# Retention attention into a gated two-layer MLP on one core: another loading, another split of small work between engines, and another order

## The chip, the cores and the metric

The kernel runs on one core of a Trainium2 chip. A core has five engines with a queue of instructions each: TensorE (PE, with its weight loads listed as PEld), VectorE (DVE), ScalarE (ACT), GpSimd (POOL) and SyncE (SP, which here only starts transfers). Each queue is worked off strictly in order, and the engines wait for each other through semaphores. SP, ACT and POOL can start transfers between DRAM and the on-chip memory SBUF; TensorE writes its results to eight banks of PSUM, from which DVE and ACT read them. The metric is the device time of one execution in microseconds.

## The reference

The first half is a linear recurrence per batch (4) and head (8), over 768 tokens with heads of 64 elements. Its output, regrouped to 512 features per token, goes through a second half:

```python
for t in range(S):                                   # gamma_h = 1 - 2**(-5-h)
    state = gamma * state + k[:, :, t] (outer) v[:, :, t]
    y[:, :, t] = q[:, :, t] . state / 8
x = y regrouped to (batch, token, 512);  x_prev = x one token earlier (0 at the first)
xk = mu_k * x + (1 - mu_k) * x_prev;   xr = mu_r * x + (1 - mu_r) * x_prev
k  = relu(xk @ w_k)                                  # 512 -> 1024
out = sigmoid(xr @ w_r) * ((k * k) @ w_v)            # 1024 -> 512
```

## The kernel before

The 4 x 768 tokens are cut into 12 blocks of 256 tokens, numbered 0 to 11, three to a batch. Within a block the recurrence is done in chunks: scores between the tokens of a chunk, a causal mask, the product with the scaled v, and a state (64 x 64 per head) carried from chunk to chunk and from block to block.

All work is written out by hand. A long string ORDER names every step, and a loop at the end of the kernel issues the steps in this order, so ORDER fixes the queue of every engine. A word is `code.block.part`, then `~engine` where the step can run on several engines (v = DVE, a = ACT, p = POOL, s = SP), and `@banks` for the PSUM banks. The codes:

- `lq`, `lk`, `lv`: load of a block's q, k, v. From POOL, q and k are turned to f16 by the transfer itself. Two loads of block 0 come from SP as f32 (the tuple EARLY) into room that the key results of blocks 1 and 2 use later, and `cq`, `ck` turn them to f16. Block 0's q and k are loaded in two halves of four heads each.
- `vs`: v times the decay, in f16 (`scale_v`, L255). `Tq`, `Tk`: transposes on TensorE (L274 with whole 128-row inputs, L280 in 64x64 pieces); `Eq`, `Ek`: their copies from PSUM to SBUF on ACT (L243).
- `S`: scores (L320, L333, L341); `M`: the mask, on DVE (L349, L356); `C`: the state's products (L368, L386, L397); `U`: running sums of the state (L421); `G`: their decay; `I`, `J`: the part of y that comes from the carried state (L443); `Y`: the part within the chunk (L464, L480, L491).
- `D`: y out of PSUM, scaled by the table gy, into xT (`yout`, L509 and L516, DVE); `dx`: x minus x_prev (`differ`, L531); `X.n.w.j`: xk (w = 0) or xr (w = 1) of a quarter of the features, from dx, mu and x_prev (`mixed`, L560, DVE).
- `K`: keys (L574, L584); `Qa`, `Qb`: relu and square on ACT (L593, L601, L605); `R` and `s`: gate and sigmoid (L614, L620); `V`: values (L626); `O`: the product with the gate (L632, DVE); `st`: the store from SP (L639). `wk`, `wr`, `wv` load weights, each w_k and w_v in two halves. `z`: products of zeros on TensorE that nobody reads (L693, L700). `gy` fills the table gy in two parts. `t` (`weighed`) is a step that no word of the ORDER before uses.

A block has one of three forms. Blocks in HALF (5 to 11) go through scores and states in chunks of 64 tokens, 64x64 at a time: one word S, one M, four U. Blocks in WIDE (2, 3, 4) use chunks of 128 tokens in layout "token p and token p+128" : two words S, two M, two U. Blocks 0 and 1 use chunks of 128 with neighbouring tokens in a row. Blocks in WHOLE (0 to 5) are transposed 128 rows at a time, the others in 64x64 pieces. GROUPS joins blocks 3 and 4, 6 and 7, 9 and 10 for the second half: one X and one K serve both.

POOL's loads are started one after another (some 0.9 us each on POOL), and in the trace never more than eight of them are under way: the next is issued when the one eight before it has landed.

Of the kernel before, what the change touches and what calls it, by code (L numbers as in the profile page):

```python
# [31 lines left out]
X.1.0.1 z.1@3 K.0.3@7 X.1.0.2 Qa.0.3 K.0.2@1 X.1.0.0 Qa.0.2 X.1.0.3 Tk.2@6 K.0.1@0 Ek.2~a vs.2~v  # L32
S.2.0@67 S.2.1@45 M.2.0~v Qb.0.3 K.1.1@1 K.1.2@2 Qa.0.1 Qb.0.2 lv.3~p C.2@0 Qa.1.2 Tq.3@3 Eq.3~a
U.2.0 I.2@67 Tk.3@0 Qa.1.1 K.1.0@2 Tq.4@1 X.1.1.0 Ek.3~a Qa.1.0 M.2.1~v Y.2 lq.5~p Eq.4~a S.3.0@45
J.2 X.1.1.1 Qb.1.0 Qb.1.2 X.1.1.2 X.1.1.3 S.3.1@23 lv.4~p K.1.3@0 Qa.1.3 Qb.1.3 wv.0~p X.0.1.3
X.0.1.2 R.0.0@1 D.2~v dx.2~v X.2.0.2 Qb.0.1 s.0.0 X.2.0.0 lq.6~p R.0.1@6 s.0.1 Tk.4@0 X.2.0.3
R.1.1@7 X.2.0.1 vs.3~p M.3.0~v Ek.4~a K.2.3@1 Qa.2.3 K.2.0@6 Qa.2.0 M.3.1~v S.4.1@45 M.4.1~v
Tq.5@1 Eq.5~a C.3@23 U.3.0~v U.3.1 s.1.1 vs.4~v R.1.0@6 s.1.0 G.3~a K.2.1@0 I.3@45 Qb.2.3 S.4.0@23
M.4.0~v Y.3 C.4@67 U.4.0 U.4.1 G.4~a K.2.2@1 Qb.1.1 I.4@23 J.3 Qa.2.1 Qa.2.2 Y.4 Qb.2.0 D.3~v
V.0.0.0@6 Tq.6@45 J.4 dx.3~v V.1.1.0@7 D.4~v dx.4~v X.3.0.1 V.0.1.0@0 V.1.0.0@1 X.2.1.2 Qb.2.2  # L40
wv.1~p V.0.0.1 Eq.6~a V.0.1.1 lq.7~p lk.6~p Tk.6@45 Ek.6~a O.0.0 Tq.7@23 Eq.7~a V.1.0.1 S.6@45
lk.5~p Tk.5@6 X.3.0.2 X.3.0.3 X.3.0.0 K.3.3@2 Qb.2.1 K.3.2@3 O.1.0 Ek.5~a O.0.1 X.3.1.1 M.6~v
lv.5~p vs.5~v K.3.5@0 Qa.3.5 Qa.3.3 K.3.4@6 V.1.1.1 Qa.3.2 lv.6~p C.5@01 S.5@45 Qa.3.4 vs.6~v
C.6@23 Qb.3.3 Qb.3.2 O.1.1 M.5~v U.5.0 X.2.1.3 U.5.1 U.6.0~a U.6.1 U.6.2 U.5.2 U.6.3 K.3.0@6
X.2.1.1 Qa.3.0 Qb.3.0 V.2.0.0@7 K.3.6@4 Qa.3.6 K.3.7@6 st.0.1 Qa.3.7 Qb.3.7 I.5@01 I.6@45 V.2.0.1
K.3.1@3 Qa.3.1 Qb.3.1 X.2.1.0 R.2.0@6 lk.8~p Tk.8@23 lv.7~p Y.5 X.3.1.0 vs.7~v X.3.1.3 Y.6 X.3.1.2
s.2.0 R.3.1@6 D.5~v dx.5~v st.1.1 st.0.0 Ek.8~a X.5.0.3 O.2.0 X.5.0.0 V.2.1.0@2 X.5.0.1 R.3.0@3
D.6~v G.6~a Qb.3.4 s.3.0 s.3.1 lv.8~p R.2.1@0 s.2.1 X.5.1.3 X.5.0.2 R.4.0@1 s.4.0 V.2.1.1 lk.7~p
C.7@67 O.2.1 lk.9~p Tk.9@01 Ek.9~a lv.11~s Tk.7@45 Ek.7~a lq.8~p U.7.0 U.7.1 U.7.2 st.2.0 vs.8~v
K.5.1@3 dx.6~v Qa.5.1 K.5.2@2 I.7@45 S.7@01 U.7.3 K.5.0@6 M.7~v lv.9~p Qb.3.6 Qa.5.0 K.5.3@3  # L50
Qa.5.2 Qb.5.0 R.4.1@6 lk.11~p Qb.3.5 vs.9~v V.4.1.0@7 X.5.1.1 C.8@01 Y.7 D.7~v dx.7~v X.6.0.3
X.6.0.0 lq.11~p Qa.5.3 Qb.5.2 Tq.8@23 X.6.0.2 V.4.1.1 s.4.1 V.4.0.0@6 Eq.8~a V.3.1.0@2 Qb.5.3
Qb.5.1 V.4.0.1 X.6.0.1 lq.9~p G.7~a V.3.0.0@3 V.3.1.1 V.3.0.1 U.8.0 K.6.3@4 Qa.6.3 O.4.0 K.6.1@5
Qa.6.1 Qb.6.1 K.6.2@6 Qa.6.2 lq.10~p O.3.1 U.8.1 st.1.0 X.5.1.0 X.5.1.2 lk.10~p U.8.2 I.8@01 O.3.0
st.2.1 Tq.9@23 Eq.9~a O.4.1 Qb.6.3 S.8@45 M.8~v K.6.0@7 K.6.6@6 Qa.6.0 Qb.6.0 Qa.6.6 X.6.1.3
S.9@23 st.3.1 Tq.11@45 Y.8 Eq.11~a X.6.1.2 R.5.1@7 s.5.1 K.6.7@6 Qb.6.2 K.6.4@4 Qa.6.4 M.9~v D.8~v
dx.8~v X.8.0.0 X.8.0.3 X.8.0.1 X.8.1.1 V.5.0.0@5 R.5.0@7 K.6.5@4 s.5.0 X.6.1.1 Tk.10@01 Qa.6.7
lv.10~p vs.10~v X.6.1.0 C.9@23 U.9.0~v Ek.10~a st.3.0 Tq.10@67 V.5.0.1 O.5.0 X.8.0.2 V.5.1.0@0
R.6.1@1 Qa.6.5 U.9.1 U.9.2 U.9.3 Eq.10~a V.5.1.1 st.5.0 O.5.1 s.6.1 Qb.6.4 S.10@45 I.9@67 C.10@23
G.9~a vs.11~v U.10.0 U.10.1 U.10.2 Qb.6.5 M.10~v st.5.1 R.6.0@1 s.6.0 R.7.0@0 s.7.0 K.8.1@1 Qa.8.1  # L60
K.8.2@2 Qa.8.2 C.11@01 I.10@45 U.10.3 Y.9 K.8.0@3 D.9~v Qb.6.7 K.8.3@2 st.4.1 Tk.11@67 G.10~a
U.11.0 U.11.1 Qa.8.0 Ek.11~a U.11.2 Y.10 D.10~v R.7.1@3 s.7.1 dx.9~v dx.10~v X.9.1.1 I.11@01
X.8.1.0 S.11@67 M.11~v X.9.0.0 Qb.8.2 V.7.0.0@4 Qa.8.3 X.9.0.2 X.9.0.1 V.7.1.0@5 V.6.0.0@3 X.9.0.3
Qb.8.1 Qb.6.6 V.6.1.0@2 V.7.1.1 X.8.1.2 V.7.0.1 V.6.0.1 V.6.1.1 K.9.5@6 K.9.7@7 Qb.8.0 st.4.0
Qa.9.5 O.6.0 Y.11 O.7.1 X.8.1.3 R.8.1@6 D.11~v dx.11~v Qa.9.7 Qb.9.7 K.9.3@5 Qb.9.5 X.11.1.3
X.11.0.1 O.6.1 X.9.1.3 V.8.1.0@7 X.9.1.2 V.8.0.0@3 X.11.0.2 st.6.1 K.9.4@0 Qa.9.4 Qb.9.4 K.9.6@1
Qa.9.6 K.9.0@2 X.9.1.0 K.9.2@0 Qa.9.2 Qb.8.3 X.11.0.3 Qb.9.2 X.11.0.0 Qa.9.3 X.11.1.0 K.9.1@1
R.9.1@0 Qa.9.1 Qb.9.1 X.11.1.2 V.8.0.1 K.11.1@5 O.7.0 Qa.11.1 R.8.0@4 V.8.1.1 Qb.9.3 s.8.0
R.10.0@5 K.11.0@1 st.6.0 Qa.9.0 Qb.9.0 st.7.1 K.11.2@2 st.7.0 R.9.0@4 Qa.11.0 Qb.9.6 Qb.11.0
Qb.11.1 X.11.1.1 O.8.0 K.11.3@1 s.9.1 V.9.1.0@3 V.10.1.0@0 s.8.1 O.8.1 st.8.1 R.11.1@6 V.9.0.0@7  # L70
Qa.11.3 V.11.0.0@1 s.10.0 Qa.11.2 Qb.11.2 R.10.1@2 V.9.1.1 O.9.1 V.10.1.1 s.10.1 O.10.1 st.9.1
Qb.11.3 V.9.0.1 st.10.1 s.11.1 Vc.11.1.1@2 s.9.0 V.10.0.0@6 O.9.0 R.11.0@0 V.11.0.1 st.8.0 st.9.0
s.11.0 Oc.11.1.1 sc.11.1.1~a O.11.0 st.11.0 V.10.0.1 O.10.0 st.10.0 Vc.11.1.0@0 Oc.11.1.0
# [716 lines left out]
```

## Time and profile before

| | |
|---|---|
| time, median of 3 runs (lowest, highest) | 156.21 us (155.82, 156.54) |
| span of the profiled execution | 154.9 us |
| granted TensorE clock in it | 1.000 |
| busy: PE, DVE, ACT, POOL | 146.0, 126.9, 99.4, 55.5 us |

The span runs from the first to the last instruction of the program; the time of a run is 1.3 us longer than this span. A busy PE is not a PE at its full pace, because a matmul counts from its start until its modelled end, and the ends overlap the next starts. The pace is read from the distance of starts instead.

### The profile page before, as it was taken

Reading aid. Unit: us, or ns where it says so; the run is one execution under the profiler, and the core shown is the slowest. Engines: PE = TensorE matmul, PEld = TensorE weight load, DVE = VectorE, ACT = ScalarE, POOL = GpSimd, SP = SyncE. Lnnn points to the kernel's source line nnn. Section 1 sums busy time; section 2 is a strip of 40 time slices with the busy share of each in tenths; the row PEclk is TensorE's granted clock in tenths of the full one; section 3 lists DMA queues with packets and bytes.
Section 4 is the critical chain, followed back from the end, with each engine's and each line's share of the span. In section 5 each row is a group of like instructions: output and inputs, shape, how many; then the busy total and the mean of one; then the engine's idle time right before and its main releaser. Section 6 shows DMA issues by size and latency. Waiting matters only on the chain.

```text
span 154.9 us, 5520 instructions
## 1 busy us (share of the span) xinstructions
PE 146.0 (94%) x2423; PEld 83.9 (54%) x2423; DVE 126.9 (82%) x205; ACT 99.4 (64%) x186; POOL 55.5 (36%) x65
## 2 busy tenths in 40 slices
...
GB/s 144 263 219 194 197 228 171 196 241 218 156 180 212 199 241 258 223 234 181 116 147 204 150 68 4 4 74 203 4 4 0 6 82 136 52 0 72 96 209 169
DMA packets 45768, 22.31 MB, mean 144 GB/s; under 512 B 37416, under 2 KB 41392, under 8 KB 45744
## 3 DMA queue, kind: packets, MB, share of 16 engines
...
q10 hardware_dynamic: 448, 0.32, 0.7%
...
## 4 chain that ended last, share of the span: by engine, by line
PE 55%; DVE 24%; DMA 12%; issue 4%; POOL 3%; DVEq 0%; POOLq 0%
PE ps L626 19%; DMA v<-in_v_dram 12%; PE ps L614 9%; PE ps L574 9%; PE ps L584 8%; DVE a L356 3%; DVE xk L560 3%; DVE xr L560 3%; DVE vs L255 3%; DVE dx L531 2%; DVE xT L516 2%; DVE tg L421 2%; DVE os L632 2%; PE ps L443 2%; DVE a L349 1%
## 5 line engine op out<-in xcount | busy, mean ns | idle before, releaser
L626 PE MATMUL ps<-wv,k2s 128*128 128x512 f16 x184 | 43.4, 379 | 0.0
L593 ACT ACTIVATE kr<-ps 128x512 f32<-128x512 f32 x48 | 27.8, 596 | 23.1 <-PE ps L574 18.0
L626 PEld LDWEIGHTS <-k2s 128*128 128x128 f16 x184 | 17.4, 98 | 20.0
L632 DVE SCALAR_TENSOR_TENSOR os<-ps,rs 128x512 f32<-128x512 f32 x23 | 15.4, 683 | 14.5 <-ACT rs L620 7.4
L614 PE MATMUL ps<-wr,xr 128*128 128x512 f16 x96 | 24.1, 380 | 0.0
L584 PE MATMUL ps<-xk,wk 128*128 128x256 f16 x192 | 24.0, 273 | 0.0
L232 POOL DMA_DIRECT2D k<-in_k_dram x20 | 17.7, 898 | 15.2 <-PE ps L280 10.5
L574 PE MATMUL ps<-xk,wk 128*128 128x512 f16 x96 | 22.5, 379 | 0.0
L584 PEld LDWEIGHTS <-wk 128*128 128x128 f16 x192 | 18.1, 98 | 4.9 <-DMA wk<-in_moe_w_k_dram 0.6
L620 ACT ACTIVATE rs<-ps 128x512 f32<-128x512 f32 x24 | 13.7, 594 | 9.3 <-PE ps L614 8.9
L560 DVE SCALAR_TENSOR_TENSOR xr<-dx,mu,xT 128x256 f16<-128x256 f32 (+1 forms) x36 | 19.2, 564 | 0.1
L560 DVE SCALAR_TENSOR_TENSOR xk<-dx,mu,xT 128x256 f16<-128x256 f32 (+1 forms) x36 | 18.8, 567 | 0.2
L232 POOL DMA_DIRECT2D v<-in_v_dram x18 | 16.2, 915 | 1.4 <-DMA q<-in_q_dram 0.5
L243 ACT COPY kT<-ps 128x1024 f16<-128x1024 f16 (+1 forms) x13 | 12.2, 947 | 5.2 <-PE ps L280 4.1
L601 ACT ACTIVATE k2s<-kr 128x512 f16<-128x512 f32 x24 | 14.9, 628 | 0.3
L574 PEld LDWEIGHTS <-wk 128*128 128x128 f16 x96 | 9.2, 98 | 10.8
L531 DVE TENSOR_TENSOR dx<-xT 128x1024 f32<-128x1024 f32 x12 | 14.6, 1223 | 0.3
L605 ACT ACTIVATE k2s<-kr 128x512 f16<-128x512 f32 x24 | 14.5, 628 | 0.1
L243 ACT COPY qT<-ps 128x1024 f16<-128x1024 f16 (+1 forms) x13 | 12.3, 949 | 2.4 <-PE ps L274 2.2
L614 PEld LDWEIGHTS <-xr 128*128 128x128 f16 x96 | 8.8, 97 | 9.2 <-DVE xr L560 0.2
L255 DVE TENSOR_TENSOR vs<-v,csm_sb 128x1024 f16<-128x1024 f32 x10 | 12.1, 1216 | 2.0 <-DMA v<-in_v_dram 2.0
L356 DVE TENSOR_TENSOR a<-ps,c_sb 128x1024 f16<-128x1024 f32 (+1 forms) x12 | 12.2, 1040 | 0.5 <-PE ps L333 0.4
...
## 6 DMA issues: line engine op xcount, KB each, us to landing
...
wk<-in_moe_w_k_dram POOLq DMA_DIRECT2D x2, 512.0 KB, 11.0
...
```

The costliest lines, as they stand in the source:

```text
L232: e.dma_start(out=dst[:, :, i * D : i * D + D], in_=src[:, i * P : i * P + P].rearrange("h p d -> p h d"),)
L243: e.copy(out=out, in_=in_)
L255: e.tensor_tensor(out=VS(n), in0=V32(n).rearrange("p h (i d) -> p i h d", i=2), in1=gks[:, int(half(n) or wide(n)), :, :, None].to_broadca ...
L356: nc.vector.tensor_tensor(out=a_full(n)[:, i, :, j0:j1], in0=pairs(banks("S", n, i, j0))[:, :, j0:j1], in1=(below if wide(n) else causal[: ...
L531: e.tensor_tensor(out=DX(k)[:, :, m * TM + t0 : m * TM + t1], in0=x[:, :, c + t0 : c + t1], in1=x[:, :, c - 1 + t0 : c - 1 + t1], op=ALU.s ...
L560: nc.vector.scalar_tensor_tensor(out=XM[w](k)[:, j, t0:t1], in0=DX(k)[:, j, t0:t1], scalar=mu[:, w * NCO + j : w * NCO + j + 1], in1=x[:, ...
L574: nc.tensor.matmul(banks("K", n, g), lhsT=wk16[:, co, g * P : g * P + P], rhs=XM[0](k)[:, co, :], start=(co == 0), stop=(co == NCO - 1),)
L584: nc.tensor.matmul(pz[:, i, :], lhsT=wk16[:, co, fo * P : fo * P + P], rhs=XM[0](k)[:, co, m * TM + t0 : m * TM + t1], start=(i == 0 and c ...
L593: nc.scalar.activation(out=kr, in_=banks("K", n, g, *u), func=AF.Relu)
L614: nc.tensor.matmul(banks("R", n, tb), lhsT=XM[1](k)[:, co, t : t + P], rhs=wr16[:, co, :], start=(co == 0), stop=(co == NCO - 1),)
L626: nc.tensor.matmul(banks("V", n, tb), lhsT=K2(n)[:, fo, tb * P : tb * P + P], rhs=wv16[:, fo, :], start=(fo == 0), stop=(fo == NFO - 1),)
L632: nc.vector.scalar_tensor_tensor(out=OS(2 * n + tb), in0=banks("V", n, tb), scalar=1.0 / (KSC * KSC), in1=RS(2 * n + tb), op0=ALU.mult, op ...
```

## The change

Block 0's q and k are now loaded by four SP loads, all as f32, and cast by DVE and ACT (EARLY has four entries). Blocks 0 and 1 are put into APART: they have no `dx`; instead ACT computes (1 - mu) * x_prev for each quarter and each of xk and xr (`t`, 16 instructions of 128x256), and DVE's X adds mu * x to it. `me` then also computes 1 - mu. HALF takes in blocks 3 and 4, WIDE keeps block 2 alone, WHOLE keeps 0, 1, 2: blocks 3, 4 and 5 are transposed in 64x64 pieces, and blocks 3 and 4 run in chunks of 64. All `vs` but block 0's go to POOL (eleven of twelve; two before), and so do `dx` of 3, 4, 5, 6, 8, 9 and 10; `dx` of 2, 7 and 11 stay on DVE. The v loads of blocks 6 to 11 go to SP (only block 11's before). gy's second part goes from ACT to DVE, four of eight G from ACT to DVE. The whole ORDER is another one; its first part is shown. In it the first keys come after the scores of block 2, and there are more words z early.

```diff
-HALF = (5, 6, 7, 8, 9, 10, 11)
-EARLY = ((1, 0, 0), (0, 0, 0))
+HALF = (3, 4, 5, 6, 7, 8, 9, 10, 11)
+EARLY = ((1, 0, 0), (0, 0, 0), (1, 0, 2), (0, 0, 2))
-APART = ()
-WHOLE = (0, 1, 2, 3, 4, 5)
-WIDE = (2, 3, 4)
+APART = (0, 1)
+WHOLE = (0, 1, 2)
+WIDE = (2,)
 ORDER = """
-lq.0.0.2~s gy.0 lv.0~p lk.0.0.2~s ck.0.0.2~v mu lk.0.2.4~p lq.0.2.4~p gy.1~a lv.1~p lk.1~p lq.1~p
-cq.0.0.2~v lq.2~p wk.0~p z.12@6 Tk.0.0.2@0 Tq.0.0.2@1 Ek.0.0.2~a Eq.0.0.2~a mt@2 wk.1~p vs.0~v
-z.2@6 S.0.0.0.2@01 me M.0.0.0.2~v S.0.1.0.2@45 Tk.0.2.4@2 M.0.1.0.2~v Tq.0.2.4@3 lk.2~p C.0@67
-U.0.0~v Ek.0.2.4~a Eq.0.2.4~a z.1@0 S.0.0.2.4@23 M.0.0.2.4~v I.0@45 S.0.1.2.4@01 M.0.1.2.4~v z.1@2
-Y.0 U.0.1 G.0~a vs.1~p Tk.1@7 Ek.1~a D.0~v dx.0~v lv.2~p lq.3~p lk.3~p C.1@01 U.1.0 X.0.0.0
-X.0.0.3 Tq.1@6 Eq.1~a z.4@2 S.1.1@67 lq.4~p X.0.0.2 I.1@45 Tq.2@0 M.1.1~v S.1.0@23 Eq.2~a wr~p
-X.0.0.1 z.1@7 K.0.0@6 M.1.0~v U.1.1 G.1~a lk.4~p Qa.0.0 X.0.1.0 X.0.1.1 Qb.0.0 Y.1 D.1~v dx.1~v
...
+mu~a lv.0~p lq.1~p lq.0.0.2~s gy.0~v cq.0.0.2~v z.12@6 Tq.0.0.2@0 lk.0.0.2~s ck.0.0.2~a lk.0.2.4~s
+Eq.0.0.2~a Tk.0.0.2@1 Ek.0.0.2~a lk.1~p gy.1~v ck.0.2.4~v z.3@2 S.0.0.0.2@01 S.0.1.0.2@23
+M.0.0.0.2~v lv.1~p mt@4 Tk.0.2.4@5 lq.0.2.4~s vs.0~v cq.0.2.4~a M.0.1.0.2~v Ek.0.2.4~a Tq.0.2.4@0
+Eq.0.2.4~a z.2@6 S.0.1.2.4@01 lv.2~p C.0@67 lk.2~p Tq.1@5 lq.2~p wk.0~p M.0.1.2.4~v U.0.0~a I.0@01
+me~a S.0.0.2.4@23 Tk.1@4 M.0.0.2.4~v Eq.1~a U.0.1~v G.0~v Y.0 D.0~v Ek.1~a S.1.0@67 M.1.0~v
+t.0.0.1~a X.0.0.1~v t.0.1.2~a vs.1~p z.4@2 z.1@2 C.1@01 U.1.0~v U.1.1~v t.0.1.0~a z.2@2 I.1@67
+S.1.1@45 M.1.1~v t.0.0.2~a X.0.0.2~v t.0.0.0~a G.1~a t.0.0.3~a Tk.2@1 Ek.2~a X.0.0.3~v X.0.0.0~v
+vs.2~p C.2@0 Y.1 D.1~v U.2.0~v Tq.2@4 Eq.2~a z.4@2 S.2.1@67 I.2@01 S.2.0@45 M.2.1~v K.0.0@2 K.0.1@3
+t.0.1.3~a t.1.0.3~a M.2.0~v Y.2 t.1.0.0~a J.2 t.1.0.1~a t.1.0.2~a Qa.0.1~a Qb.0.1~a t.1.1.2~a wk.1~p
+K.0.2@3 X.1.0.0~v X.1.0.1~v t.1.1.1~a X.1.0.2~v Qa.0.2~a X.1.0.3~v K.1.1@4 K.1.0@3 X.0.1.0~v D.2~v
+t.1.1.3~a t.0.1.1~a K.1.3@5 Qa.0.0~a K.0.3@2 Qb.0.0~a t.1.1.0~a Qa.1.0~a Qa.1.3~a X.0.1.2~v
...
     def whole(n):
-        return n in WHOLE or n in WIDE
+        return n in WHOLE
```

The two steps that the change brings into use, both there before:

```python
    def weighed(e, n, w, j, i=None):                       # t
        nc.scalar.activation(
            out=lagged(n, w, j, t0, t1), in_=x[:, j, c - 1 + t0 : c - 1 + t1], func=AF.Copy,
            scale=nu[:, w * NCO + j : w * NCO + j + 1])    # nu = 1 - mu, room of dx
    def mixed(e, n, w, j, i=None):                         # X, for blocks in APART
            nc.vector.scalar_tensor_tensor(
                out=XM[w](k)[:, j, t0:t1], in0=x[:, j, c + t0 : c + t1],
                scalar=mu[...], in1=lagged(n, w, j, t0, t1), op0=ALU.mult, op1=ALU.add)
```

More of the change, by code (lines that the diff above doesn't have):

```diff
@@ L32 @@
[L32 to L73, printed above, removed]
@@ L74 @@
-sc.11.1.0~s
+mu~a lv.0~p lq.1~p lq.0.0.2~s gy.0~v cq.0.0.2~v z.12@6 Tq.0.0.2@0 lk.0.0.2~s ck.0.0.2~a lk.0.2.4~s
[4 more added lines that the diff above has]
+t.0.0.1~a X.0.0.1~v t.0.1.2~a vs.1~p z.4@2 z.1@2 C.1@01 U.1.0~v U.1.1~v t.0.1.0~a z.2@2 I.1@67
@@ new lines @@
+S.1.1@45 M.1.1~v t.0.0.2~a X.0.0.2~v t.0.0.0~a G.1~a t.0.0.3~a Tk.2@1 Ek.2~a X.0.0.3~v X.0.0.0~v
[3 more added lines that the diff above has]
+t.1.1.3~a t.0.1.1~a K.1.3@5 Qa.0.0~a K.0.3@2 Qb.0.0~a t.1.1.0~a Qa.1.0~a Qa.1.3~a X.0.1.2~v
+X.0.1.3~v X.0.1.1~v X.1.1.2~v Qb.1.3~a dx.2~v Qa.1.1~a lv.3~p Qa.0.3~a K.1.2@3 Qb.1.1~a wr~p R.0.0@5
@@ new lines @@
+X.2.0.0~v s.0.0~a lk.3~p lq.3~p X.2.1.1~v X.1.1.1~v X.1.1.0~v R.0.1@4 X.1.1.3~v R.1.0@2 Tq.3@01
+s.0.1~a vs.3~p X.2.0.3~v Qa.1.2~a wv.0~p Eq.3~a X.2.0.1~v lv.4~p Tk.3@45 C.3@67 Ek.3~a s.1.0~a
+wv.1~p X.2.1.0~v X.2.0.2~v X.2.1.2~v U.3.0~v U.3.1~v U.3.2~v R.1.1@3 s.1.1~a Qb.1.0~a K.2.1@0
+Qa.2.1~a Qb.1.2~a K.2.0@6 Qa.2.0~a I.3@23 S.3@45 Qb.0.3~a K.2.2@1 V.0.1.0@0 V.1.0.0@6 lk.4~p U.3.3~v
+G.3~a M.3~v Y.3 D.3~v X.2.1.3~v V.1.1.0@7 Qb.0.2~a V.0.1.1 O.0.1~v st.0.1~s V.1.0.1 O.1.0~v lq.4~p
+lv.5~p Qa.2.2~a lk.5~p Qb.2.0~a vs.4~p Tk.4@01 Ek.4~a C.4@23 U.4.0~v lk.7~p lk.6~p Tq.4@45 Eq.4~a
@@ new lines @@
+R.2.1@6 s.2.1~a K.2.3@0 Qa.2.3~a U.4.1~v U.4.2~v U.4.3~v lq.5~p vs.5~p G.4~a I.4@23 S.4@45 M.4~v
+dx.3~p V.0.0.0@6 V.0.0.1 Qb.2.1~a Qb.2.3~a O.0.0~v Y.4 D.4~v C.5@45 Tk.5@01 V.1.1.1 O.1.1~v Ek.5~a
+Qb.2.2~a V.2.1.0@6 st.0.0~s V.2.1.1 lq.6~p R.2.0@7 Tq.5@23 U.5.0~v U.5.1~v U.5.2~v O.2.1~v lv.6~s
+dx.4~p X.3.0.1~v X.3.0.2~v X.3.0.0~v s.2.0~a lq.7~p Eq.5~a X.3.0.3~v Tk.6@45 Ek.6~a Tk.7@01
+X.3.1.2~v V.2.0.0@7 V.2.0.1 O.2.0~v Ek.7~a K.3.7@4 Qa.3.7~a Tq.6@01 Eq.6~a lq.9~p X.3.1.1~v I.5@23
+lv.7~s S.5@67 M.5~v K.3.4@4 vs.6~p Qa.3.4~a K.3.2@5 lk.8~p S.6@67 Qb.3.7~a X.3.1.0~v vs.7~p
```

32 lines of the change are left out of this document (added).

## The prediction

> **What bounds the kernel now.** I read the page's busy line first, then five stages, then the distances of matmul starts.
>
> ```profile
> PE 146.0 (94%) x2423; PEld 83.9 (54%) x2423; DVE 126.9 (82%) x205; ACT 99.4 (64%) x186; POOL 55.5 (36%) x65
> 0.00:25.00 25.00, 20.77 (x377) 12.82 (x378) 19.09 (x40) 14.11 (x29) 19.67 (x26) 1.00 1.37 205
> 25.00:45.00 20.00, 19.15 (x315) 13.60 (x314) 18.82 (x27) 15.63 (x31) 13.87 (x16) 1.00 1.47 199
> 45.00:130.00 85.00, 84.74 (x1614) 45.69 (x1612) 82.28 (x130) 56.85 (x105) 21.98 (x25) 1.00 0.80 128
> 151.30:154.90 3.60, 0.00 (x0) 0.00 (x0) 0.42 (x1) 0.00 (x0) 0.00 (x0) 1.00 0.47 172
> ```
>
> The columns are stage, length, busy PE, PEld, DVE, ACT, POOL, clock, DMA, GB/s. From 45 us on TensorE (PE) never rests, though VectorE (DVE) is busy 97% of the time. The pace of needed PE work I take from starts:
>
> ```profile
> 29.54 0.64 PE L274 MATMUL ps<-c_sb,q 128*64 128x128 f16 x16
> 30.01 0.61 PE L480 MATMUL ps<-a,vs 128*64 128x128 f16 x16
> 30.55 0.40 PE L333 MATMUL ps<-qT,kT 64*128 64x128 f16 x8
> 50.29 0.45 PE L280 MATMUL ps<-c_sb,k 64*64 64x64 f16 x32
> 50.57 0.44 PE L280 MATMUL ps<-c_sb,q 64*64 64x64 f16 x32
> 50.94 1.04 PE L626 MATMUL ps<-wv,k2s 128*128 128x512 f16 x4
> 125.33 4.32 PE ps L574 x20
> ```
>
> A whole transpose takes 0.47 us (29.54 to 30.01), one in pieces 0.28 (50.29 to 50.57), with 0.10 more where a full matmul follows (50.57 to 50.94). A 128x512 matmul takes 0.216 (4.32/20), one of 256 half. Needed work: 376 x 0.216 + 208 x 0.109 = 103.9; transposes 8.9, scores 4.7, states 2.9, the products for y 7.5; 31 changes from small to full matmuls 3.1. Sum 131.0. What is left up to the last matmul's end at 151.3 is "lost" (idle, or zeros): 20.2. It is 13.4 when the second key step begins (21.5 us), 14.9 at 31.5, 16.6 at 45.9, 20.1 at 130. The end after the last matmul is 3.6. So a change pays through less needed work or less lost time; DVE, ACT and POOL count only through these. The sum is made against the 154.9 us span; the median of 156.2 is 1.3 more.
>
> **Needed work.** Three blocks turn 2 x 3 transposes from 0.47 to 0.27: -1.2. Blocks 3 and 4 in 64-token form: scores 0.46 to 0.27 each, -0.4; products for y about -0.2; states equal. In the new order 28 changes to full matmuls instead of 31: -0.3. Together -2.1, to 128.9.
>
> **Engines' loads.** Rows for the prices:
>
> ```profile
> L255 DVE TENSOR_TENSOR vs<-v,csm_sb 128x1024 f16<-128x1024 f32 x10 | 12.1, 1216 | 2.0 <-DMA v<-in_v_dram 2.0
> L255 POOL TENSOR_TENSOR vs<-v,csm_sb 128x1024 f16<-128x1024 f32 x2 | 3.8, 1918 | 3.7 <-DMA v<-in_v_dram 3.6
> L531 DVE TENSOR_TENSOR dx<-xT 128x1024 f32<-128x1024 f32 x12 | 14.6, 1223 | 0.3
> L356 DVE TENSOR_TENSOR a<-ps,c_sb 128x1024 f16<-128x1024 f32 x8 | 9.7, 1218 | 0.5 <-PE ps L333 0.4
> L560 DVE SCALAR_TENSOR_TENSOR xk<-dx,mu,xT 128x256 f16<-128x256 f32 x24 | 10.5, 478 | 0.1
> L243 ACT CAST tg<-ps 128x256 f16<-128x256 f32 x1 | 0.4, 391 | 0.0
> q1 hardware_dynamic: 1056, 0.52, 9.0%
> ```
>
> DVE: nine vs x 1.22 = -11.0; nine dx (two dropped, seven to POOL) x 1.22 = -11.0; two masks -2.4; four U more +1.7; four G and gy's part +2.4. About 20 less, 107. ACT: sixteen t; no row has them, so between 0.32 (the 128x128 of gy, 1.28/4) and 0.60 (128x512), I take 0.39 by the 128x256 cast: +6.3; two casts +1.2; four G (1.06 each) and gy -5.5: about 101. POOL: nine vs x 1.92 = +17.3; seven dx, unseen there, between DVE's 1.22 and twice a POOL vs, 3.84; I take 1.92, the same size: +13.4; ten v loads and two q/k loads of block 0 less, -10.7: 75. SP gets those v loads behind stores in its queue; block 11's landed 6 us after issue there, and v6 (issued near 49) would land by 56, wanted by vs.6 at 54: small.
>
> **The first 25 us, where keys begin later.** The last row above covers 0 to 20 us: 0.52 MB of f32 through SP took 9% of 20 us, 1.8 us of all DMA engines. As much comes on top now, in front of or beside POOL's queue: between 0 (it replaces two halves on POOL, which landed 1.2 apart) and 1.8 us of delay. POOL's landings were 1.45 apart for a q or k, 1.5 for v (2.2 in two pieces), 1.8 for k in pieces, 2.6 for a weight half. v0 landed at 8.14; now I take 8.9 (half of the bounds). Then q1 11.0, k1 12.5, v1 14.0, v2 16.2, k2 18.1, q2 19.5, first half of wk 22.1 (17.8 before). POOL is held by vs.1 (14.0 to 15.9) and vs.2 (16.3 to 18.2); wk's second half is issued behind them and lands at 24.6.
>
> PE waits in order: Tq.1 11.0, Tk.1 12.5, Y.0 13.1, C.1 16.0 (vs.1), Y.1 19.0, Tq.2 19.6, S.2.0 22.2, first key 22.5. DVE behind it: M.0 to 12.6, D.0 to 15.0, M.1 to 19.0, three X to 20.4, D.1 to 21.6, U, M.2.1 and M.2.0 to 24.45; then Y.2, and K.0.2 at 25.2. Needed work by then is 10.15: lost 15.0, against 13.8 before at 25.
>
> **25 to 45 us.** Here ACT is the tight engine. After Qa.0.1 at 24.45 its queue runs without a rest: squares 0.63, relus 0.60, t 0.39. K.1.2 waits 0.3 for Qa.1.0, R.1.0 waits 0.7 for block 1's last X, which DVE ends at 33.6 (it has D.2, dx.2 and three X of block 2 in front). Lost 16.5 at Tq.3 (34.5) and, with three small waits for the sigmoids and Qa.2, 17.2 at 45 us, against 16.6 before. wr (29.4), q3 (32.6), wv (35.2 and 40.0), k4 (41.8) land a little before they are wanted, so they cost nothing at this pace, but all that front would gain is taken up by them.
>
> **45 us to the end.** Before lost 3.5 more here. DVE falls from 82 to about 66 busy us of 85 (seven vs and seven dx less, three G more), ACT has room. New waits are short: dx.4 on POOL ends at 53.6, X.3.0 at 56.6, K.3.7 is wanted at 57.0. I take 3.0. Sum: 128.9 + 17.2 + 3.0 + 3.6 = 152.7, 2.2 less than 154.9: 154.0 us as a time.
>
> **The rivals.** *Front late.* The SP loads take the full 1.8, and t is 0.60: 16 x 0.2 = 3.3 on the tight ACT queue, of which half reaches PE. Lost +0.9 (the half I left out) + 1.7, so 156.6: about no change. For it: DMA is over 90% busy from 4 us on; against: zeros stand in the new order just where my walk has gaps, so the order allows for the waits that my walk has, and no others.
>
> *POOL and DVE hold each other up (slower).* vs, dx and X read two SBUF operands. In this profile POOL's two vs ran at 11.0 and 37.0, beside masks and U that read one operand from PSUM; so no row shows what an X does beside a POOL multiply. Free to fully exclusive, one costs DVE 0 to 1.92. Fourteen of the eighteen lie after 45 us, where DVE has 85 - 66 = 19 us of room: it decides from 1.4 us each on. At 1.92 DVE needs 66 + 27 = 93, 8 more than the stage: about 162; at 1.65 each 4 more, 158. At 0.96 each (13 us) DVE is as busy as before, and the forecast stands. The Trainium skill ("SBUF — State Buffer", section "Who interferes with whom") has exactly this: a VectorE instruction with two SBUF inputs and a GpSimd one that reads SBUF exclude each other for a whole instruction. By that rule 1.92 is the most that one can cost, and only where an X is next; no run here shows it yet.
>
> *Front on time.* SP's loads slip between POOL's at no cost, and ACT's t at 0.32: lost -0.9 and -0.6 (half of 16 x 0.07), so 152.5.
>
> **How the numbers follow.** Forecast 0.45 (own range 152.9 to 155.4), front on time 0.13, front late 0.22, POOL against DVE 0.20 (157.2 to 162). A measurement tells about 0.5%, 0.8 us. Faster (under 155.4): 0.45 + 0.13 = 0.58, less 0.02 for the forecast's upper end, 0.56. Slower (over 157.0): 0.20 and a quarter of the late front, 0.25. Same: 0.19. Both signs hold much, so the range is 152.0 to 158.5; above it are the dearer half of the POOL rival, and below it little.
>
> **What would show it.** First key step near 22.5 us, 17.2 lost at 45; transposes of blocks 3 to 5 at 0.28; DVE near 107 busy, POOL 75. Wrong: X or POOL's vs and dx longer than 0.48 and 1.9 where they meet; PE idle after 45 us before K.3, K.5 or K.6; the first key after 24 us.

## The result, and the profile after

The changed kernel takes 173.73 us (173.48 to 174.05, four runs) against 156.11 for the kernel before on the same chip: a ratio of 1.1136, 95% interval 1.1106 to 1.1165. The forecast was 154.0 with a range up to 158.5. It is wrong in sign and by almost 20 us. Runs over 1.5% longer than the fastest of the same kernel are left out of the times and ratios below, but three profiles (v of blocks 6 to 10 by POOL; fills with the old front, without and with v by POOL) are of such runs.

One slip in the texts above belongs here first: they say that seven differences `dx` go to GpSimd (POOL). The order moves five (3, 4, 5, 6 and 8), as the rows below show; POOL has 16 such steps, not 18. With five, the forecast's own sums would be 109 us for DVE and 71 for POOL, where it has 107 and 75.

The page of the changed kernel, its first lines and the tenths of TensorE (PE), VectorE (DVE) and clock:

```profile
span 172.3 us, 6000 instructions
PE 151.2 (88%) x2651; PEld 85.3 (50%) x2651; DVE 122.1 (71%) x197; ACT 102.7 (60%) x186; POOL 73.7 (43%) x67
PE   7939889789799988397995499999999999999990
DVE  2363999996276999399969979997799984102141
PEclk9965999999999999879999569999999999999998
```

A slice is 4.3 us. PE rests in the third (8.6 to 12.9 us), the 17th (69 to 73) and the 22nd and 23rd (90 to 99), and the clock is low in or behind each. Before, PE never rested after 45 us. DVE was to be busy 107 us and is busy 122. The stages, with the columns of the prediction's first fence:

```profile
0.00:25.00 25.00, 19.92 (x339) 11.05 (x339) 14.78 (x33) 12.65 (x25) 18.65 (x23) 0.86 1.19 204
25.00:45.00 20.00, 17.32 (x288) 12.21 (x288) 16.34 (x30) 16.77 (x33) 16.01 (x17) 1.00 1.47 203
45.00:130.00 85.00, 75.81 (x1821) 41.94 (x1820) 72.12 (x104) 52.46 (x92) 39.00 (x29) 0.94 0.85 118
```

From 45 to 130 us PE is busy 75.8 instead of 84.7 of 85 us, while DVE, the engine that was busiest, is busy 72.1 instead of 82.3: 13 us of room, and yet the time went here. Which DVE steps changed their length is in the groups kept apart by shape, the first line from the kernel before, the others from the changed one:

```profile
L560 DVE SCALAR_TENSOR_TENSOR xk<-dx,mu,xT 128x512 f16<-128x512 f32 x12 | 8.3, 745 | 0.1
L566 DVE SCALAR_TENSOR_TENSOR xk<-dx,mu,xT 128x512 f16<-128x512 f32 x12 | 13.3, 1157 | 1.8 <-POOL dx L537 1.8
L566 DVE SCALAR_TENSOR_TENSOR xk<-dx,mu,xT 128x256 f16<-128x256 f32 x16 | 7.2, 479 | 0.0
L436 DVE TENSOR_TENSOR tg<-t,csm_sb 128x256 f16<-128x256 f32 x4 | 4.8, 1195 | 0.1
L261 POOL TENSOR_TENSOR vs<-v,csm_sb 128x1024 f16<-128x1024 f32 x11 | 21.8, 1988 | 6.0 <-DMA v<-in_v_dram 2.9 <-PE ps L590 2.9
L537 POOL TENSOR_TENSOR dx<-xT 128x1024 f32<-128x1024 f32 x5 | 10.6, 2117 | 27.4 <-DVE xT L515 27.4
```

The wide X took 745 ns before and takes 1157 in the mean; G on DVE takes 1195 where a step of its size takes 420. Taken one by one, eight DVE steps are long (the others have their old length), 11.7 us in excess in sum. The timeline of DVE from 88 to 100 us, and POOL's in the same stretch (start, length, engine, step, count):

```profile
90.72 3.06 DVE L566 SCALAR_TENSOR_TENSOR xk<-dx,mu,xT 128x512 f16<-128x512 f32 x2 [1.78 <-POOL dx L537]
94.48 1.93 DVE L566 SCALAR_TENSOR_TENSOR xr<-dx,mu,xT 128x256 f16<-128x256 f32 x1
97.54 3.05 DVE L566 SCALAR_TENSOR_TENSOR xk<-dx,mu,xT 128x512 f16<-128x512 f32 x2
```
```profile
87.82 2.87 POOL L537 TENSOR_TENSOR dx<-xT 128x1024 f32<-128x1024 f32 x1 [8.36 <-DVE xT L515]
94.18 1.94 POOL L261 TENSOR_TENSOR vs<-v,csm_sb 128x1024 f16<-128x1024 f32 x1
97.85 2.18 POOL L261 TENSOR_TENSOR vs<-v,csm_sb 128x1024 f16<-128x1024 f32 x1
```

An X of 0.47 lasts 1.93 beside a `vs`; two of 0.74 last 3.05 together. What that does to PE is in the timeline of PE, as is a stop of another kind 25 us earlier:

```profile
71.87 0.36 PE L449 MATMUL ps<-qT,tg 64*64 64x64 f16 x10 [2.84 <-issue]
97.07 1.44 PE L632 MATMUL ps<-wv,k2s 128*128 128x512 f16 x3 [4.17 <-DVE os L638]
```

At 97.07 PE has waited 4.17 us for O (`os`), which stood behind two stretched X in DVE's queue. The stop before 71.87 is marked issue: PE, DVE and ACT wait for nothing that the profile shows.

The prediction's measure, lost time at PE (start of a step less the needed work up to it), puts the places in order. It is 18.6 at the first key step (26.30 us), 22.8 at 47.9 us, 39.1 at the end; before it was 16.6 at 45.9 and 20.1 at the end. The large rises behind 45 us: +1.2 at 65 us (X stretched), +3.05 at 72 (the stop) and +0.8 behind it at a low clock (0.66 from 70 to 75 us), +1.1 at 82 (G stretched), +4.3 at 97 (two X and O), +2.6 up to 102 (another X, clock 0.55 from 95 to 100). After 105 us it rises by 1.0.

### The profile page after: what moved, and what is told of

It is laid out like the page before. It is cut to its first block, busy times and chain, and to the rows that moved or that the text cites. A ratio compares the mean times of both kernels' runs of the same rounds, so it can differ in the third digit from the quotient of the medians.

```text
span 172.3 us, 6000 instructions
## 1 busy us (share of the span) xinstructions
PE 151.2 (88%) x2651; PEld 85.3 (50%) x2651; DVE 122.1 (71%) x197; ACT 102.7 (60%) x186; POOL 73.7 (43%) x67
## 4 chain that ended last, share of the span: by engine, by line
PE 65%; DVE 15%; ACT 6%; DMA 5%; issue 4%; POOL 2%; SPq 1%; DVEq 0%; POOLq 0%
PE ps L632 20%; PE ps L580 12%; PE ps L620 11%; PE ps L590 9%; DMA k2s<-in_q_dram 5%; DVE xk L566 4%; PE ps L286 2%; DVE xk L560 2%; DVE a L362 2%; PE ps L449 2%; PE ps L280 2%; ACT dx L550 2%; PE ps L326 2%; POOL dx L537 2%; DVE xT L515 2%
## 5 line engine op out<-in xcount | busy, mean ns | idle before, releaser
L632 PE MATMUL ps<-wv,k2s 128*128 128x512 f16 x184 | 44.6, 385 | 4.2 <-DVE os L638 4.2
L590 PE MATMUL ps<-xk,wk 128*128 128x256 f16 x192 | 25.5, 279 | 1.7 <-ACT kr L599 1.0
L580 PE MATMUL ps<-xk,wk 128*128 128x512 f16 x96 | 25.6, 405 | 0.9 <-DVE xk L566 0.9
L261 POOL TENSOR_TENSOR vs<-v,csm_sb 128x1024 f16<-128x1024 f32 x11 | 21.8, 1988 | 6.0 <-DMA v<-in_v_dram 2.9
L590 PEld LDWEIGHTS <-wk 128*128 128x128 f16 x192 | 18.8, 100 | 8.3 <-issue 3.2
L537 POOL TENSOR_TENSOR dx<-xT 128x1024 f32<-128x1024 f32 x5 | 10.6, 2117 | 27.4 <-DVE xT L515 27.4
L566 DVE SCALAR_TENSOR_TENSOR xk<-dx,mu,xT 128x256 f16<-128x256 f32 (+1 forms) x28 | 20.5, 769 | 1.9 <-POOL dx L537 1.8
L566 DVE SCALAR_TENSOR_TENSOR xr<-dx,mu,xT 128x256 f16<-128x256 f32 (+1 forms) x28 | 18.2, 667 | 0.0
L515 DVE TENSOR_TENSOR xT<-ps,gy_sb 128x512 f32<-128x512 f32 x18 | 12.4, 690 | 6.1 <-PE ps L449 5.1
L580 PEld LDWEIGHTS <-wk 128*128 128x128 f16 x96 | 9.5, 103 | 11.2 <-issue 2.4
L355 DVE TENSOR_TENSOR a<-ps,c_sb 128x1024 f16<-128x1024 f32 x9 | 11.0, 1221 | 5.1 <-PE ps L326 5.1
```

The lines of the kernel that those rows point to most:

```text
L261: e.tensor_tensor(out=VS(n), in0=V32(n).rearrange("p h (i d) -> p i h d", i=2), in1=gks[:, int(half(n) or wide(n)), :, :, None].to_broadca ...
L515: nc.vector.tensor_tensor(out=x[:, :, :, v], in0=banks("I", n)[:, v].rearrange("p (j i t) -> p j i t", j=NJ, i=2), in1=g[:, :, :, v], op=A ...
L566: nc.vector.scalar_tensor_tensor(out=XM[w](k)[:, j, t0:t1], in0=DX(k)[:, j, t0:t1], scalar=mu[:, w * NCO + j : w * NCO + j + 1], in1=x[:, ...
L580: nc.tensor.matmul(banks("K", n, g), lhsT=wk16[:, co, g * P : g * P + P], rhs=XM[0](k)[:, co, :], start=(co == 0), stop=(co == NCO - 1),)
L590: nc.tensor.matmul(pz[:, i, :], lhsT=wk16[:, co, fo * P : fo * P + P], rhs=XM[0](k)[:, co, m * TM + t0 : m * TM + t1], start=(i == 0 and c ...
L632: nc.tensor.matmul(banks("V", n, tb), lhsT=K2(n)[:, fo, tb * P : tb * P + P], rhs=wv16[:, fo, :], start=(fo == 0), stop=(fo == NFO - 1),)
```

## The experiments

Theory A: a POOL multiplication or subtraction and a DVE step with two SBUF operands hold each other up, and PE waits for the stretched step. Theory B: POOL's steps come late because POOL works in order. Theory C: block 0's loads by SP put the front late. Kernels built on the changed kernel are compared with its 173.73, kernels built on the one before with its 156 to 157; ratios are all to the kernel before on the same chip.

**POOL's steps back on DVE.**

```diff
-vs.2~p ... vs.4~p ... vs.11~p
+vs.2~v ... vs.4~v ... vs.11~v
-dx.3~p dx.4~p dx.5~p dx.6~p dx.8~p
+dx.3~v dx.4~v dx.5~v dx.6~v dx.8~v
```

> The changed kernel with nine multiplies of v (blocks 2 and 4 to 11) and the five differences dx back on DVE; loads, forms and order as changed. Theory A (a GpSimd multiply and a DVE step with two SBUF inputs shut each other out): the mixes X are 0.48 and 0.74 us again wherever GpSimd no longer multiplies, the waits of TensorE near 63 to 66, 80 to 82 and 92 to 102 us shrink, 173.7 falls by 7 to 11, to 163 to 167 us. Rival B (the loss is late loads and late data; DVE has no room for this work): DVE gets 17 us more to do and the time stays at 172 to 177 us.

178.33 us, ratio 1.1406 (1.1243 to 1.1569). One stretched step is left (0.9 us in excess), so the stretching does hang on POOL's steps. But the kernel is slower still. PE's waits (who waits, for whom, us in sum, times, the longest) have two sorts in it:

```profile
PE ps L374 <- DVE vs L261: 3.8, 3, 1.5
PE ps L449 <- issue: 3.4, 1, 3.4
```

The steps stand in DVE's queue at places that were POOL's, and DVE, which takes them without a rest, comes to them late: PE waits for `vs` before C.2 (3.0), C.4 and C.10 (1.5 each) and C.11 (0.8). The 3.4 us before C.6, and 1.6 before C.8, are no waits for DVE but stops marked issue, like the one at 69 us in the changed kernel. The run says nothing of the price of the stretching.

**Block 0's second halves from POOL again, as f16.**

```diff
-EARLY = ((1, 0, 0), (0, 0, 0), (1, 0, 2), (0, 0, 2))
+EARLY = ((1, 0, 0), (0, 0, 0))
-lk.0.2.4~s ... ck.0.2.4~v ... lq.0.2.4~s ... cq.0.2.4~a
+lv.0~p lk.0.2.4~p lq.0.2.4~p
```

> The changed kernel with the second halves of block 0's q and k loaded by GpSimd as f16 again, behind its v, and their casts gone. Theory C (the f32 loads by SP wait behind GpSimd's packets, and hold up DVE, which has the cast in front of the first mask): the first mask starts by 8.5 us instead of 9.8, first key step near 23.5 instead of 26.3, time 170 to 171.5 us. Rival (the front hangs on q, k and v of block 1, which come no earlier): first key after 25.5 and a time of 173 us or more.

170.70 us, ratio 1.0917 (1.0781 to 1.1053): 3.0 us less, as theory C had it. The first key step begins at 23.7 instead of 26.3, and lost time when block 2 is scored (S.2.1) falls from 18.3 to 15.7. It had been 4.7 less just before C.1; there a stop of 2.2 us marked issue takes half of the gain. The stretched steps are all still there, with +4.3 again before V.3.1.0.

**v of blocks 6 to 10 loaded by POOL.** This is `lv.6~s` to `lv.10~s` turned to `~p`.

> The changed kernel with the v loads of blocks 6 to 10 on GpSimd again. Theory D (the pause of TensorE of 2.8 us at 69 us, for nothing that the profile names, and the slow clock behind it come from TensorE's instructions being fetched late while SP's v loads crowd the DMA engines): the pause is below 0.5 us, clock 1.0 at 70 to 75 us, time 168.5 to 170.5 us. Rival (the pause has another cause, or GpSimd, with 9 us of issuing more, is late with its multiplies): pause stays, or the time is 173 us or more.

171.26 us in the one run that counts (the profiled one took 173.84), so no gain is established. The stop at 69 us was gone, but waits of 2.3 and 2.5 stood nearby, behind an X and a G of 3.3 us each. This left the stop's cause open.

**Ten idle POOL multiplications in the kernel before, and ten fills.** Each multiplies a buffer of 1024 elements that is free at that time by a table, both in SBUF, and nothing waits for it; the second kernel fills the same 1024 f32 and reads nothing.

```diff
+    def probe(e):
+        e.tensor_tensor(out=f, in0=f, in1=gks[...], op=ALU.mult)   # first kernel
+        e.memset(V32(8), 0.0)                                      # second kernel
-lv.10~p
+lv.10~p pp~p pp~p pp~p pp~p pp~p pp~p pp~p pp~p pp~p pp~p
```

> The kernel before, with ten idle GpSimd multiplies of 1024 elements (both inputs in SBUF, nobody reads the result) behind its last load, from about 81 us on. Theory A: DVE's mixes that meet one last up to 2.4 us instead of 0.48 and 0.74, steps that read PSUM (masks, U, O) keep their length, GpSimd's multiplies that meet a mix are longer than 1.95; the time is 157 to 165 us. Rival (they do not disturb each other): all mixes 0.47 to 0.75 us, 156 us.

> As the probe with ten multiplies, but GpSimd writes zeros over the same 1024 elements ten times and reads nothing. Theory A (what shuts the two out is GpSimd reading through the same way as DVE's second operand): all of DVE's mixes are 0.47 to 0.75 us, the time is that of the kernel before, 155.5 to 157 us. Rival (any GpSimd work of that kind disturbs DVE, or the ten instructions cost through something else): mixes longer than 1 us again, time above 158 us.

170.16 us with the multiplications (one run) and 155.98 with the fills (one run), against 156.67 and 156.38. DVE's four wide X in the timeline of the first, and of the second:

```profile
86.16 9.19 DVE L566 SCALAR_TENSOR_TENSOR xk<-dx,mu,xT 128x512 f16<-128x512 f32 x4
```
```profile
80.81 10.13 POOL L261 MEMSET v<- 128x1024 f32 x10
82.30 2.74 DVE L563 SCALAR_TENSOR_TENSOR xk<-dx,mu,xT 128x512 f16<-128x512 f32 x4
```

2.30 us for an X beside the multiplications, 0.69 beside the fills. So it isn't that POOL is busy, but that it reads SBUF while DVE has two operands there. The kernel with the multiplications is 13.5 us longer, but not all of that is their price. 2.0 us are lost before the first of them starts: v of block 0 landed at 8.87 instead of 8.14, and with the front later an X of block 1 met the `vs` at 36 us and took 2.12. 11.4 us are lost behind it, for ten steps that nobody needs. In this run and the others, the DVE steps stretched by 0.5 us or more are X, G, `vs` and `dx`, which have two operands in SBUF; masks, U and O, which read one of theirs from PSUM, keep their length.

**The kernel before with the fourteen steps on POOL, nothing else changed.**

```diff
-vs.2~v ... vs.4~v ... vs.11~v ... dx.3~v dx.4~v dx.5~v dx.6~v dx.8~v
+vs.2~p ... vs.4~p ... vs.11~p ... dx.3~p dx.4~p dx.5~p dx.6~p dx.8~p
```

> The kernel before, with the same fourteen steps as in the change moved to GpSimd (v of blocks 2 and 4 to 11, differences of 3, 4, 5, 6, 8), nothing else. Theory A: mixes of up to 2.4 us and G, vs and dx beside them longer, ten or more DVE steps stretched by 1 us and more; the time is 163 to 175 us. Rival B (in the change the order and the loads make the loss): DVE falls by 14 us of work, and the time is 154 to 159 us.

186.48 us, ratio 1.1924 (1.1839 to 1.2009), outside both forecasts, and by theory B's mechanism: only one stretched step (1.07). Two lines of the waits (who waits, for whom, us in sum, times, the longest):

```profile
POOL vs L255 <- DMA v<-in_v_dram: 22.5, 8, 5.9
POOL dx L531 <- DVE xT L509: 15.8, 2, 13.3
```

POOL also issues the loads. While it waits for v or for xT, the k, q and v of later blocks aren't asked for, and PE loses 7.7, 5.8 and 6.6 us at three places. In the changed kernel the order was written for these steps, and this loss is small there: POOL waits 27.4 us for xT, but with loads issued ahead.

**The four SP loads and casts alone, in the kernel before.**

```diff
-EARLY = ((1, 0, 0), (0, 0, 0))
+EARLY = ((1, 0, 0), (0, 0, 0), (1, 0, 2), (0, 0, 2))
-lk.0.2.4~p lq.0.2.4~p ... Tk.0.2.4@2 ... Tq.0.2.4@3
+lk.0.2.4~s lq.0.2.4~s ... ck.0.2.4~v Tk.0.2.4@2 ... cq.0.2.4~a Tq.0.2.4@3
```

> The kernel before, with the second halves of block 0's q and k loaded by SP as f32 and cast (k on DVE, q on ACT), nothing else. Theory C (SP's f32 loads come late beside GpSimd's packets): the halves land at 9.5 to 11.5 us instead of 8.6 and 9.3, v of block 0 at 9 to 9.5 instead of 8.1, and the time is 1 to 3 us longer, 157 to 159 us. Rival (a load by SP is at least as quick): 155 to 156.5 us.

161.82 us, ratio 1.0348 (1.0323 to 1.0372), more than theory C's 157 to 159. The second half of k lands at 8.48 and of q at 11.75, where POOL's landed at 8.57 and 9.32; the first key step begins at 22.7 instead of 18.4, lost time there is 17.0 instead of 12.7, and it is never won back.

**Blocks 3 and 4 in 64-token form, in the kernel before.** HALF takes in 3 and 4, WIDE keeps 2, and the words of these blocks in the order are put together anew.

> The kernel before, with blocks 3 and 4 in chunks of 64 tokens (transposes as before, a few words of the order moved for it), nothing else. By the sum of the prediction the needed TensorE work falls by 0.6 us and DVE's by 0.7; if TensorE's work sets the time from 45 us on, 155.2 to 156.0 us, 0.2 to 0.6 us faster than before. Rival (the two further sums of the state per block and the order eat it): 156 to 157 us.

162.80 us, ratio 1.0382 (1.0344 to 1.0421). By the prices of the prediction needed work falls by 0.6, to 130.4, but lost time is 27.6, and 6.8 of the 7.3 in excess stand at five words around blocks 3 and 4 which I had to place. The longest of these waits, 2.3 us before V at 52.4 us, is another stop marked issue. The run says nothing of the form itself.

**Fills in place of POOL's reading steps, in the changed kernel.** This takes the reading away and leaves order, queue and lengths (two fills take 1.94 us, a `vs` 1.99).

```diff
     def scale_v(e, n):
+        if e is nc.gpsimd:
+            e.memset(V32(n), 0.5); e.memset(VS(n), 0.02); return
     def differ(e, n, i=None):
+        if e is nc.gpsimd:
+            e.tensor_copy(out=d[:, :, 0:1], in_=x[:, :, c + t0 : c + t0 + 1])
+            e.memset(d, 0.01); e.memset(d, 0.01); return
```

> The changed kernel with its order and its division of the engines, but every multiplication of v (blocks 1 to 11) and the five differences that are GpSimd's are replaced by two fills of the same size that write and read nothing (a fill of 1024 f32 took 1.01 us in the earlier probe, so about 2.0 for two); of the differences a four-element copy stays, to keep their wait. What v and these differences would give is therefore left out of the output, the times of the steps stay. Theory A (GpSimd's reading of SBUF holds up VectorE's X): the eight stretched steps go, and with them the growth of lost time behind them, 1.2 + 1.35 + 1.2 + 1.1 + 4.3 and what TensorE's low clock adds after each: 162 to 167 us, X all at 0.48 or 0.75. Rival B (the steps are late because GpSimd works in order, whatever they read): 171 or more, VectorE waiting where it was stretched.

165.81 us, ratio 1.0589 (1.0533 to 1.0644), 7.9 less than the changed kernel and in the range of theory A. Its groups by shape:

```profile
L576 DVE SCALAR_TENSOR_TENSOR xk<-dx,mu,xT 128x512 f16<-128x512 f32 x12 | 8.4, 747 | 0.1
L440 DVE TENSOR_TENSOR tg<-t,csm_sb 128x256 f16<-128x256 f32 x4 | 1.7, 420 | 0.1
L262 POOL MEMSET v<- 128x1024 f32 x11 | 10.7, 971 | 7.1 <-DMA v<-in_v_dram 7.0
```

No DVE step is stretched, and the 1.8 us that X waited for a `dx` of POOL are gone as well. Lost time is 30.1 instead of 39.1. It still rises by 3.3 at the stop and 2.5 behind it, at a lower clock.

**The same with the front as before.** Both edits, of the fills and of block 0's halves, together.

> The same with block 0's second halves of q and k loaded by GpSimd as f16 again. Theory C with A (the late front and the held-up X are two causes that add up; the front alone gave 3.0): 159 to 164 us, first key step at 23 us. Rival (what the front gives is taken up by a later wait once X is free): within 1 us of the run with the fills alone. What is then left over 156 is the pause at 69 us and the waits of the order itself.

Ratio 1.0385 (1.0304 to 1.0466), which is 162.6 us against 156.57: the two causes add up. The stop stays, 3.04 us.

**No differences in blocks 0 and 1, alone, in the kernel before.**

```diff
-APART = ()
+APART = (0, 1)
-dx.0~v ... dx.1~v ... X.0.0.0
+t.0.0.0~a X.0.0.0          # and so for the sixteen X of both blocks
```

> The kernel before with one part of the change alone: no differences in blocks 0 and 1, ScalarE makes the sixteen weighed columns t there (0.44 each in the changed kernel, 7 us), VectorE drops two differences (2.4 us). Theory: ScalarE is the tight engine up to 45 us, so about half of its 7 us reaches TensorE: 157.5 to 160.5. Rival: ScalarE has the room (busy 78% from 25 to 45 us) and VectorE's 2.4 us are saved: 154.5 to 156.5.

167.66 us, ratio 1.0709 (1.0646 to 1.0771), above both forecasts. The waits say why:

```profile
DVE xr L554 <- ACT dx L544: 7.4, 5, 2.3
```

and 3.2 us more for xk. Each `t` stood in ScalarE's queue just ahead of its X, behind squares and transposes' copies, and VectorE, which has no rest there, waited for it. In the changed order the `t` come earlier, and DVE's rows for these X show 0.1 us of idle time ahead of them. So these 11 us are the price of a place, not of the step.

**The stop: SP's loads of v, taken away or put in.** First the fills and the old front with `lv.6` to `lv.10` on POOL; then the kernel before with these five on SP.

> The kernel of the last but one run (fills for GpSimd's reading steps, front as before) with v of blocks 6 to 10 loaded by GpSimd again; the output lacks v and five differences as there. Theory D (the pause of 3.0 us at 68 us is TensorE's sequencer waiting for instructions while SyncE's five f32 loads of v fill the DMA engines): the pause and the low clock behind it (0.78 from 70 to 74 us) go, 4 to 5 us: 157 to 159.5. Rival (the pause belongs to the program's size and order, whoever loads): still a gap of 2 to 3 us near 68 us marked issue, 161 or more.

> The kernel before with v of blocks 6 to 10 loaded by SyncE, nothing else changed. Theory D: TensorE gets a pause of 2 to 4 us marked issue while these loads run (45 to 90 us) and the low clock behind it: 158.5 to 162. Rival (such loads alone cost nothing, as the prediction had it): 155.5 to 157, no such pause.

The first: ratio 1.0359 (1.0297 to 1.0421), 162.0 us, no better than with the loads on SP, and the stop is still there (2.2 us). The second: 159.25, ratio 1.0199 (1.0134 to 1.0265), with no stop at all; its lost time is 3.2 more already when block 1 is scored (S.1.1 begins at 18.8 instead of 15.6 us), before the first of the moved loads is issued at 28.6, so its 2% are not explained by them either. Behind 45 us it loses nothing against the kernel before. That its time lies in theory D's range is luck: the stop that the theory asks for isn't there. Theory D falls.

**The stop: a place in the program, or a wait of the word.** In all kernels of the changed order but one, PE stopped after the same number of recorded instructions. So one key step was moved ahead of that place.

```diff
-Y.5 D.5~v ... C.6@01 U.6.0~v U.6.1~v K.3.6@4 U.6.2~v
+K.3.6@4 Y.5 D.5~v ... C.6@01 U.6.0~v U.6.1~v U.6.2~v
```

> The run with fills and the old front, and one key step of block 3 (four full matmuls, 0.87 us) moved from behind C.6 to before Y.5, where TensorE stood still for 3.0 us. Theory E (TensorE runs out of instructions at one place of its program, the 2497th recorded one, until a 16 KB fetch has come): it still stops at that number, now three instead of seven matmuls into Y.5's second part, and about 0.9 us shorter, 2.0 to 2.4; the whole 161 to 163 us. Rival (something that this word waits for, its operands or its PSUM banks): it stops where it did, after seven matmuls, or not at all.

164.31 us, ratio 1.0527 (1.0479 to 1.0575). PE's timeline with the fills alone, and with the key step moved:

```profile
65.86 0.24 PE L453 MATMUL ps<-qT,tg 64*64 64x64 f16 x6
69.15 0.37 PE L453 MATMUL ps<-qT,tg 64*64 64x64 f16 x10 [3.05 <-issue]
```
```profile
66.17 0.22 PE L453 MATMUL ps<-qT,tg 64*64 64x64 f16 x3
68.92 0.28 PE L453 MATMUL ps<-qT,tg 64*64 64x64 f16 x11 [2.52 <-issue]
```

With eight instructions (four matmuls and their weights) put ahead, PE stops four matmuls earlier than in its sister with the old front, which stopped after seven, and for 2.5 us instead of 3.0. The stop is a little longer than theory E's 2.0 to 2.4, and the time is above its 161 to 163. But it isn't the word that waits: in each of these kernels PE stops right behind its 2497th recorded instruction. So it was in all seven kernels of the changed order that show the stop. The DMA records show what comes then: a fetch of 16 KB on the instruction queue (20 of these in the changed kernel's span). PE goes on 2.3 to 2.6 us after the start of that fetch in all seven. In five it starts 0.2 to 0.9 us behind the beginning of the stop, in one 0.2 ahead; in the run with the old front alone it starts 1.0 ahead, and the stop is 1.4 us. In the kernel without a stop there (POOL loads v, POOL multiplies) it had started 148 instructions earlier.

The traces hold more of these stops. In all sixteen kernels together, behind the first 12 us, PE stands still 28 times for 0.5 us or more with nothing but issue named. In the kernel with the key step moved it does so three times ahead of the stop at 66 us:

```profile
PE ps L407 <- issue: 1.3, 1, 1.3
PE ps L474 <- issue: 1.1, 1, 1.1
PE ps L330 <- issue: 0.9, 1, 0.9
```

The 28 lie right behind the recorded instructions (matmuls, weight loads and a few of PE's sequencer, in order of time) 449, 705, 1217, 1729, 2241, 2497, 2753, 3265 and 3777, and any two of these numbers differ by a whole multiple of 256. In all 28 PE goes on 2.2 to 3.0 us after a fetch has started. 16 KB for 256 instructions would be 64 bytes for each, so one fetch seems to bring one such stretch (an estimate from these two numbers). So PE ran out of instructions at the end of a stretch, and a stop lasts as long as the next fetch is late. 27 of the 28 are in kernels of the changed order, the other is in the kernel before with blocks 3 and 4 in 64-token form (behind the 1729th); the kernel before has none. Both run more matmuls than the kernel before (2651 and 2551, not 2423), and the added ones are small. That this makes the stops is not shown.

Why a fetch is started so late stays open; before the stop at the 2497th instruction PE ran 320 to 440 recorded instructions in 5 to 9 us since the fetch before, in the kernels where it is long, where the mean is some 260 for a fetch.

## Why the prediction was wrong

*Needed work, 131.0 less 2.1.* Right. 128.9, the lost 39.1 and 3.6 behind the last matmul make 171.6 of the span of 172.3. All of the miss is lost time: forecast 17.2 + 3.0, measured 39.1, 18.9 more.

*"POOL and DVE hold each other up", chance 0.20, 157 to 162.* This was the mechanism, and the largest part: 9.0 us of lost time, 7.9 of the time of a run, between the changed kernel and the one with fills. Two steps of its pricing failed. First "it decides from 1.4 us each on", since DVE had 19 us of room after 45 us: the 16 steps cost DVE 11.7 us in excess, 0.73 each, which by that rule would have left the forecast standing. Room in a stage's sum isn't slack at a place. PE takes its steps in order, and a stretched X or O that is wanted next reaches PE at once, while the room lies elsewhere: DVE idled 13 of those 85 us. Behind the long waits the clock fell as well (0.55 from 95 to 100 us, 0.77 from 100 to 105), which no term of the sum held. Second "one costs DVE 0 to 1.92": a G of 0.42 took 3.00, 2.58 more. The reason to give the rival a low chance, that no row showed an X beside a POOL multiplication, was a reason for the middle of the bounds, not for their lower end. The Trainium skill's rule ("SBUF — State Buffer", section "Who interferes with whom") is that a VectorE step with two SBUF inputs contends with a GpSimd step that reads SBUF and not with one that only writes it. The runs agree on both halves: 2.30 us beside multiplications, 0.69 beside fills.

*The first 25 us, lost 15.0 at K.0.2.* Measured 18.8. The delay of v0 was taken as half of 0 to 1.8 and was 1.4 (landing 9.55, forecast 8.9), within its bounds. What failed is the walk behind it: it prices what SP's loads do to POOL's, but has no landing for the second halves of k and q themselves. They landed at 9.73 and 11.51, where POOL's landed at 8.57 and 9.32 in the kernel before. The chain of waits has that load as its longest piece:

```profile
2.32 9.19 DMA k2s<-in_q_dram
```

Behind it the clock fell to 0.52 from 10 to 15 us. Everything then came 0.6 to 1.4 later than forecast (k1 13.6 for 12.5, v2 17.2 for 16.2), the second half of wk 1.8 (26.4 for 24.6). The "front late" rival named these loads and added 0.9 for them; putting the loads back gave 3.0, and in the kernel before the loads alone cost 5.4.

*25 to 45 us, ScalarE as the tight engine, +2.2.* Measured +4.0, of which an X stretched from 0.47 to 2.13 at 28.4 us made 1.2; two waits of 0.7 at K.0.3 and K.1.2, and 1.2 at K.2.2, of which 0.9 is a stop marked issue (behind the 1217th instruction), are the rest. `t` was taken as 0.39 and is 0.44 (7.0 us for sixteen), a small miss. The load of ACT, 101 forecast, is 102.7.

*45 us to the end, 3.0.* Measured 16.3. Besides the stretching it held the stop at the 2497th instruction, 3.05 and some 0.8 to 1.6 behind it at the low clock; no row of the prediction shows such a stop, and no rival had it. With the fills, the old front and the key step moved, 28.1 us are lost, 7.9 more than forecast for the whole kernel: 4.3 are this stop and what follows, and 3.6 are left. The three earlier stops of that kernel, at C.1, K.2.2 and C.5, raise lost time by 1.4, 1.1 and 1.3, which is as much as these 3.6. So a term for the supply of instructions, which the sum did not have, is what is left of the miss.

*v6 by SP by 56 us, "small".* It landed at 62.0, since its issue came at 57 instead of 49. That it is small held: with v on POOL again the time was the same within its interval.

The 18.9 us then are 9.0 of stretching, 2.0 of the front, 4.3 of the stop at the 2497th instruction and 3.6 that other stops of its kind account for, by the differences of the lost time in the profiles on the way from the changed kernel (39.1) over the fills (30.1) to the last kernel (28.1) and the forecast (20.2). Each kernel has its own stops (the old front brings one at C.1 that the changed kernel hasn't), so the 2.0 is what is left of a larger gain. Single terms differ by a microsecond or two with where v0 happens to land: 8.8 to 9.8 us in the five kernels with SP's four loads, 7.2 to 8.9 in the others.

The signs of being wrong that the prediction names all came: X of up to 2.39 beside POOL's steps, PE idle before K.3 at 64 us, the first key at 26.3. No version with a part of the change beats the kernel before.
